# Transposing Q, K and x in the DMA crossbar instead of on TensorE, in an attention-and-feed-forward kernel

## The chip, the cores and the metric

One core of one Trainium2 chip. The metric is the time of one execution in device microseconds (us), median of several executions. Every timed series ran together with the kernel before on the same chip, and ratios compare only those runs. Some executions fall into a slower state (a lower granted TensorE clock, over 1.5% above the fastest of the same kernel). They are marked slow and left out of ratios.

The views of the profile use short names: PE is TensorE (PEld its weight loads), DVE is VectorE, ACT is ScalarE, POOL is GpSimd, SP is SyncE, which issues transfers. "Crossbar" stands for the transposing transfer that `dma_start_transpose` asks of the DMA engines. The span is the time from the first to the last instruction of a profiled execution. The granted clock is the share of TensorE's full speed that was allowed.

## The reference

Four batches of eight heads, 768 tokens, head size 64. Attention is causal with a window of 128 keys plus four sink keys; the result goes through a feed-forward stage with three first-layer matrices joined by a maximum.

```python
keep = is_sink | in_window                 # n_sink = 4, window = 128
a = softmax(where(keep, q @ k.T / sqrt(64), -1e9))
x = (a @ v) as [3072 tokens, 512]
h = maximum(maximum(x @ w1, x @ w2), x @ w3)    # 512 -> 768
out = h @ w_out                                 # 768 -> 512
```

Inputs and output are float32; the kernel computes in bf16 with float32 sums.

## The kernel before

The tokens are cut into 12 chunks of 256 (three per batch). A software pipeline runs in the loop: iteration i does the first layer and output of chunk i, the attention of chunk i+1, the K and Q preparation of chunk i+2, and it issues the load of chunk i+3. The order on every engine is the order in which the program emits instructions; the program asks for no scheduler. The parts that the change touches:

```python
def prep(ci, j, g):                       # K (j=0) or Q (j=1), 4 heads
    x = bfs[ci]                           # bf16, cast by GpSimd
    pt = ps_o.tile([128, 2, 2, 128], BF16, tag="o", name="pt")
    for i in range(2):
        for p in range(2):
            nc.tensor.transpose(..., x[:, j, g, i, p * 128:(p + 1) * 128], ident)
    if j == 1:                            # Q: ACT copies out of PSUM
        put(nc.scalar.copy, qT[...], slice(0, 128))
    else:                                 # K: DVE copies each head of a pair into
        for h in range(2):                # its own half of kz, rest of kz is zero
            put(nc.vector.tensor_copy, kz[...][:, 2 * g:2 * g + 2, h], hp)
        if c == 0 and b > 0:
            sink_k(b, g)                  # DVE copies the sink keys of a new batch
# ... (cut)
def xpose(ci, t):                         # x, 128 tokens
    for ds in range(DS):                  # DS = 4
        nc.tensor.transpose(pt[:, ds], x[:, ds * 128:(ds + 1) * 128], ident)
    nc.scalar.copy(xTs[ci][:, :, t * 128:(t + 1) * 128], pt)
# ... (cut)
for i in range(2, NCH):                   # letter, chunk (a=i, b=i+1, c=i+2), index
    cast(i + 2)                           # GpSimd
    load(i + 3)                           # SyncE: 6 to 10 DMAs
    run("Sb0 Fa0 Sb1 Fa1 Sb2 Fa2 Sb3 Kc0 Fa3 Zb Sb4 Fa4 Ab00 Sb5 Qc0 Fa5 Ab01 Sb6 Kc1 Fa6 "
        "Sb7 Qc1 Fa7 Fa8 Ab10 Ab11 Ya0 Tb0 Tb1 Ya1", a=i, b=i + 1, c=i + 2)
```

S is the score of one head, F one of nine groups of eight first-layer matmuls, Z the scores against the sink keys, A attention times V, T the transposes of x, Y the output with its store, K and Q the preparation above. Sink keys are the first four keys of a batch, which every query sees; they are kept in a tile of their own, ks.

The softmax here doesn't subtract the row's maximum and nothing guards it: scores larger than these inputs give would overflow.

## Time and profile before

| | kernel before |
|---|---|
| time of its first three runs | 211.73 us (211.26 to 212.39) |
| span of the profiled run, granted clock | 208.2 us, 1.00 |
| TensorE (PE) busy | 191.0 us, 92% |
| loop, first h matmul of chunk 3 to that of chunk 11 | 123.4 us, 15.4 per iteration |

How to read it: the prediction below shows the lines that make PE the bound. Two more views are needed. First, the queues of the DMA engines from the page (packets, MB, then the time that the packets took as a share of 16 engines over the span; in a table by stretch a packet counts where it starts, so that a share there can pass 1):

```profile
q1 hardware_dynamic: 73984, 25.21, 47.8%
```

Second, the timeline of SyncE, which issues nearly all transfers, over one iteration (start, duration, destination and source, count):

```profile
102.86 0.36 SPq L329 DMA_DIRECT2D out_dram<-y_sb  x1
103.31 1.20 SPq L80 DMA_DIRECT2D qk_raw<-in_k_dram  x2
...
107.90 1.24 SPq L85 DMA_DIRECT2D v_raw<-in_v_dram  x2
115.42 2.54 SPq L329 DMA_DIRECT2D out_dram<-y_sb  x2
```

SyncE issues ten loads in 5.8 us and is then idle for 6.3 us, until the next stores.

### The profile page before, as it was taken

The page shows a single profiled execution, that of the slowest core. Times are in us where ns is not written, and L with a number is a line of the kernel's source. Part 1 is how long each engine was busy: PE and PEld are TensorE (multiplying, and loading weights), DVE is VectorE, ACT ScalarE, POOL GpSimd, SP SyncE. Part 2 cuts the span into 40 slices and gives each one's busy share as a digit, 9 for nine tenths or more (in the row PEclk, how much of TensorE's full clock was granted, in tenths as well). Part 3 has the DMA queues.
Part 4 walks back from the last instruction along what each step waited for, and adds up shares of the span by engine and source line. Part 5 has one row for each costly group of instructions (what it writes and reads, how often), then busy time and mean ns, then how long its engine had stood idle before and what let it go on. Part 6 is the DMA issues. An engine that isn't in the chain of part 4 may idle for free.

```text
span 208.2 us, 5083 instructions
## 1 busy us (share of the span) xinstructions
PE 191.0 (92%) x2027; PEld 155.2 (75%) x2039; DVE 131.2 (63%) x289; ACT 117.0 (56%) x216; POOL 66.1 (32%) x110
## 2 busy tenths in 40 slices
PE   7664879899899999999999999999999999999992
PEld 7553768785687798688587798798687797796870
DVE  3787516995488288299288288298299288276250
ACT  8766751444763764764653764764653863863412
POOL 6289119978245143025024043024025000000000
PEclk9999999999999999999999999999999999999998
DMA  5999996972999393385295392392284200200202
GB/s 135 231 264 203 215 258 115 242 170 103 209 280 220 121 219 69 107 181 117 76 220 115 116 228 63 113 229 65 102 193 111 104 0 3 101 5 0 104 0 101
DMA packets 76391, 28.67 MB, mean 138 GB/s; under 512 B 65872, under 2 KB 73296, under 8 KB 76368
## 3 DMA queue, kind: packets, MB, share of 16 engines
q1 hardware_dynamic: 73984, 25.21, 47.8%
q0 software_dynamic: 2384, 3.15, 8.9%
q8 instruction: 16, 0.26, 0.6%
q14 instruction: 7, 0.06, 0.1%
HBM read 25.20 MB, written 6.29 MB: 151 GB/s over the span
## 4 chain that ended last, share of the span: by engine, by line
PE 68%; DVE 18%; ACT 9%; issue 2%; POOL 0%; DVEq 0%; POOLq 0%; ACTq 0%
PE h_ps L313 37%; PE y_ps L324 9%; DVE h_sb L319 6%; DVE e_sb L254 6%; DVE x_sb L289 4%; ACT e_sb L251 4%; PE st L244 4%; PE pt L207 4%; PE o_ps L281 3%; PE xt_ps L301 2%; PE warm L117 2%; PE st L245 2%; ACT h_sb L317 2%; PE sk L260 2%; PE st L242 1%
## 5 line engine op out<-in xcount | busy, mean ns | idle before, releaser
L313 PE MATMUL h_ps<-xT,w 128*128 128x256 bf16 x864 | 107.9, 273 | 0.7 <-ACT xT L302 0.7
L313 PEld LDWEIGHTS <-w 128*128 128x128 bf16 x864 | 81.1, 98 | 9.5 <-issue 0.8
L251 ACT ACTIVATE e_sb<-st 128x512 bf16<-128x512 f32 (+1 forms) x96 | 53.6, 565 | 23.5 <-PE st L245 23.5
L319 DVE TENSOR_TENSOR h_sb<-h_sb,h_ps 128x512 bf16<-128x512 bf16 x72 | 49.4, 686 | 18.0 <-PE h_ps L313 15.1
L254 DVE TENSOR_TENSOR e_sb<-e_sb,msk 128x1024 bf16<-128x1024 bf16 (+1 forms) x48 | 33.7, 703 | 41.1 <-ACT e_sb L251 40.9
L186 POOL CAST qk_bf<-qk_raw 128x512 bf16<-128x512 f32 x36 | 24.6, 688 | 68.8 <-DMA qk_raw<-in_k_dram 49.6
L327 ACT COPY y_sb<-y_ps 128x512 f32<-128x512 f32 x24 | 14.1, 586 | 35.9 <-PE y_ps L324 32.9
L324 PE MATMUL y_ps<-wo,h_sb 128*128 128x512 bf16 x132 | 33.1, 379 | 0.7
L317 ACT CAST h_sb<-h_ps 128x512 bf16<-128x512 f32 x36 | 21.1, 586 | 17.1 <-PE h_ps L313 16.9
L244 PE MATMUL st<-qT,kz 128*128 128x256 bf16 x96 | 25.8, 273 | 2.0 <-DVE kz L215 1.0
L324 PEld LDWEIGHTS <-h_sb 128*128 128x128 bf16 x144 | 12.5, 98 | 12.7 <-DVE h_sb L319 2.7
L289 DVE TENSOR_TENSOR x_sb<-o_ps,rc 128x256 bf16<-128x256 f32 x48 | 20.4, 425 | 1.7
L245 PE MATMUL st<-qT,kz 128*128 128x128 bf16 x96 | 20.9, 219 | 0.0
L281 PE MATMUL o_ps<-ve,e_sb 128*128 128x65 bf16 x352 | 18.6, 193 | 1.9 <-DVE e_sb L254 1.9
L190 POOL CAST ve<-v_raw 128x512 bf16<-128x512 f32 x24 | 15.6, 656 | 12.9 <-DMA v_raw<-in_v_dram 12.7
L281 PEld LDWEIGHTS <-e_sb 128*128 128x128 bf16 x352 | 16.6, 97 | 3.8 <-DVE e_sb L254 2.5
L207 PE MATMUL pt<-ident,qk_bf 128*128 128x128 bf16 x192 | 18.3, 221 | 1.2 <-DVE kz L213 0.6
L215 DVE COPY kz<-pt 64x512 bf16<-64x512 bf16 x40 | 16.7, 418 | 3.4 <-PE pt L207 3.0
L207 PEld LDWEIGHTS <-qk_bf 128*128 128x128 bf16 x192 | 12.7, 99 | 2.9 <-issue 1.2
L242 PE MATMUL st<-qT,kz 128*128 128x128 bf16 x64 | 14.0, 219 | 0.0
L302 ACT COPY xT<-xt_ps 128x512 bf16<-128x512 bf16 x24 | 13.3, 595 | 0.8 <-PE xt_ps L301 0.8
L244 PEld LDWEIGHTS <-kz 128*128 128x128 bf16 x96 | 9.4, 98 | 3.7 <-DVE kz L215 1.3
(48 smaller groups left out, 135.4 us busy)
## 6 DMA issues: line engine op xcount, KB each, us to landing
v_raw<-in_v_dram SPq DMA_DIRECT2D x24, 256.0 KB, 4.3
out_dram<-y_sb SPq DMA_DIRECT2D x24, 256.0 KB, 2.0
qk_raw<-in_k_dram SPq DMA_DIRECT2D x40, 128.0 KB, 2.8
qk_raw<-in_q_dram SPq DMA_DIRECT2D x36, 128.0 KB, 2.8
w<-in_moe_w_dram POOLq DMA_DIRECT2D x3, 768.0 KB, 11.3
qk_raw<-in_q_dram SPq DMA_DIRECT2D x6, 256.0 KB, 4.2
qk_raw<-in_k_dram SPq DMA_DIRECT2D x4, 256.0 KB, 4.2
wo<-in_moe_w_out_dram POOLq DMA_DIRECT2D x2, 384.0 KB, 5.6
```

The source lines that it names most:

```text
L186: eng.tensor_copy(bfs[ci][:, j, g].rearrange("p i x -> p (i x)"), qk[:, j, g])
L207: nc.tensor.transpose(pt[:, i, p] if runs else pt[:, p, i], x[:, j, g, i, p * 128:(p + 1) * 128], ident)
L244: nc.tensor.matmul(st[:, 1:3], lhsT=kh[:, 0:128], rhs=qh, start=True, stop=True)
L245: nc.tensor.matmul(st[:, 3], lhsT=kh[:, 128:256], rhs=qh[:, 128:256], start=True, stop=True)
L251: nc.scalar.activation(e[:, h, lo:], st[:, lo:], AF.Exp, scale=scale)
L254: nc.vector.tensor_tensor(out=e[:, :, lo:], in0=e[:, :, lo:], in1=m, op=ALU.mult)
L281: nc.tensor.matmul(o[:, hh], lhsT=es[ci, p][:, h, sl], rhs=ve[b % 2][:, n, 2 * p + h], start=(c == 0 and x == 0), stop=(x == len(blocks) - 1),
L289: nc.vector.tensor_mul(xs[ci, t][:, 4 * g:4 * g + 4], o[:, :, 0:D], rc.unsqueeze(2).to_broadcast([128, 4, D]))
L313: nc.tensor.matmul(hp[:, f], lhsT=w_sb[wi][:, ds, (2 * fp + f) * 128:(2 * fp + f + 1) * 128], rhs=xTs[ci][:, ds, :], start=(ds == 0), stop ...
L317: nc.scalar.copy(dst, hp)
L319: nc.vector.tensor_max(dst, dst, hp)
L324: nc.tensor.matmul(yp, lhsT=hs[ci][:, fb, t * 128:(t + 1) * 128], rhs=wo[:, fb], start=(fb == 0), stop=(fb == FB - 1))
```

## The change

Intent: take 24 of PE's transposes out of each iteration and give them to the DMA crossbar. K is written zero-padded in bf16 by GpSimd, so that the crossbar fills the padded tile directly and DVE's copies go as well. Queries stay in two-token order (a partition holds two neighbouring tokens, so the even tokens come first and then the odd ones), which lets Q be loaded in 512-byte runs; the stores put the rows back in place. The order of the loop is new, so that x is ready earlier.

```diff
 def cast_qk(ci, j, g, eng):
+    if j == 0 and ci >= CPB:                    # K, zero-padded, into kb
+        for h in range(2):
+            eng.tensor_copy(kb[ci % 2][:, 2*g:2*g+2, h, :, 64*h:64*h+64]..., qk[:, j, g]...)
+        return
 ...
 def prep(ci, j, g):
+    if ci >= CPB:
+        if j == 0 and g == 0:
+            nc.sync.dma_start_transpose(out=kz[...], in_=kb[ci % 2]...)      # 0.52 MB
+        elif g == 0:
+            nc.sync.dma_start_transpose(out=qT[...], in_=bfs[ci][:, 1]...)   # 0.26 MB
+        return
-        if c == 0 and b > 0:
-            sink_k(b, g)
 def sink_score(ci):
+    if c == 1 and b > 0:                        # sink keys copied directly ahead of Z
+        for g in range(2):
+            sink_k(b, g)
 def xpose(ci, t):
+    if ci >= CPB:
+        nc.sync.dma_start_transpose(out=xTs[ci][:, t], in_=xs.pop((ci, t))...)
+        return
 def ffn_y(ci, t):
-    nc.sync.dma_start(out=out[r0:r0 + 128], in_=y)
+    for i in range(2):
+        nc.sync.dma_start(out=...[i], in_=y[64 * i:64 * i + 64])
 # entry of the loop
+run("Kd0 Qd0", d=3)
 load(4)
-run("Ac10 Ac11 Yb0 Tc0 Kd0 Tc1 Qd0 Yb1 Kd1 Qd1", b=1, c=2, d=3)
+run("Ac10 Ac11 Yb0 Tc0 Tc1 Yb1", b=1, c=2)
 # loop: cast(i + 2); load(i + 3); then
-    run("Sb0 Fa0 Sb1 Fa1 Sb2 Fa2 Sb3 Kc0 Fa3 Zb Sb4 Fa4 Ab00 Sb5 Qc0 Fa5 Ab01 Sb6 Kc1 Fa6 "
-        "Sb7 Qc1 Fa7 Fa8 Ab10 Ab11 Ya0 Tb0 Tb1 Ya1", ...)
+    run("Kc0 Qc0 Sb0 Fa0 Sb1 Sb2 Fa1 Sb3 Zb Sb4 Fa2 Sb5 Ab00 Fa3 Sb6 Ab01 Sb7 Fa4 Fa5 Ab10 "
+        "Tb0 Ab11 Tb1 Fa6 Fa7 Fa8 Ya0 Ya1", ...)
```

Cut: masks and score operands for the two-token order, K of chunks 1 and 2 loaded in 256-byte instead of 512-byte runs, the clearing of kb in place of kz.

## The prediction

> **What bounds the kernel now.** I read the engine shares first, then the table by stretch cut at the iterations of the steady loop, then the timeline of one iteration, then the groups of what is removed, and last the waits and the queue of SyncE, because the new transposes are issued there.
>
> ```profile
> PE 191.0 (92%) x2027; PEld 155.2 (75%) x2039; DVE 131.2 (63%) x289; ACT 117.0 (56%) x216; POOL 66.1 (32%) x110
> ...
> 117.20:132.90 15.70, 15.54 (x173) 12.97 (x173) 10.10 (x22) 9.54 (x19) 4.29 (x6) 1.00 0.54 135
> 132.90:148.70 15.80, 15.60 (x172) 12.76 (x172) 10.90 (x26) 9.45 (x19) 4.04 (x6) 1.00 0.54 134
> 148.70:163.30 14.60, 14.28 (x150) 11.54 (x150) 9.90 (x22) 8.43 (x18) 4.04 (x6) 1.00 0.58 144
> ```
>
> The last three lines are one iteration each of the loop (span, then busy us of PE, weight loads, DVE, ACT, POOL, then granted clock, DMA share, GB/s). PE is busy for all but 0.2 to 0.3 us of each, at full clock. Busy could still hide waits, so I check it against what PE must stream. In the chain of waits eight h matmuls of 256 columns take 0.87 us, that is 109 ns each, and six of 512 columns 1.29 us. In the timeline one head's scores take 0.22 us and one group of nine attention matmuls 0.44. An iteration whose attention chunk is not the first of its batch then needs 9 x 0.87 (h) + 8 x 0.22 (scores) + 0.44 (sink scores) + 4 x 0.44 (attention) + 2 x 1.29 (y) + 16 K and Q transposes at 0.055 (0.88) + 8 x transposes (0.44) = 15.7 us. Measured: 15.7 and 15.8. So the loop (55.0 to 193.6 us, nine such iterations) is bound by PE's issue, and 1.32 us of each is transposes.
>
> ```profile
> L207 PE MATMUL pt<-ident,qk_bf 128*128 128x128 bf16 x192 | 18.3, 221 | 1.2 <-DVE kz L213 0.6
> L301 PE MATMUL xt_ps<-ident,x_sb 128*128 128x128 bf16 x96 | 9.6, 221 | 2.6 <-DVE x_sb L289 1.3 <-ACT xT L302 0.7
> L215 DVE COPY kz<-pt 64x512 bf16<-64x512 bf16 x40 | 16.7, 418 | 3.4 <-PE pt L207 3.0
> L302 ACT COPY xT<-xt_ps 128x512 bf16<-128x512 bf16 x24 | 13.3, 595 | 0.8 <-PE xt_ps L301 0.8
> PE sk L260 <- DVE ks L229: 2.8, 1, 2.8
> POOL qk_bf L186 <- DMA qk_raw<-in_k_dram: 49.6, 15, 9.9
> 118.05 1.00 SPq L80 DMA_DIRECT2D qk_raw<-in_k_dram  x2
> out_dram<-y_sb SPq DMA_DIRECT2D x24, 256.0 KB, 2.0
> ```
>
> The 221 ns of a transpose is its pipeline length, not its cost: pieces of the chain show eight in 0.45 us. The 2.8 us is the only long PE wait: the first sink score waits for DVE's sink-key copies. POOL waits only for loads, so casts run an iteration ahead. A SyncE issue of a load takes 0.5 us, of a store 0.36.
>
> **What the Trainium skill says.** "VectorE: DVE Perf Modes", section "The three transpose paths", gives 390 ns for a 128x128 transpose on TensorE and 1309 ns through the DMA crossbar: worse by latency, but on another unit. "TensorE: Matmul & The Clock Gate", section "Part 4: PE-mode transpose", has about 275 ns in a kernel; the trace has 221, and only 55 in occupancy. "DMA: Bandwidth & Descriptors", section "Latency and other measured facts", has 261 GB/s for a DMA transpose. No transfer in the trace before is a transpose; its plain loads in 256-byte packets reach 229 GB/s at a DMA share of 0.99, which is near it. The same page, "Issuing engines are not separate DMA queues": all DMAs share 16 engines, so transposes queue among the loads; the trace agrees in that loads land in 2.8 us alone and 14 at worst.
>
> **The change, part by part.**
>
> PE: the order of instructions has 432 fewer on PE, 216 transposes with their weight loads: 9 chunks x 16 (K, Q) and 9 x 8 (x). 216 x 0.055 = 11.9 us, all on the bound, plus about 0.1 us of waiting for x per iteration. With no new wait the floor is 14.4 us for an ordinary iteration and 13.0 for one whose chunk begins a batch: 6 x 14.4 + 3 x 13.0 = 125.4 us where the loop now has 138.6. This is the most that the loop can give, 13 us.
>
> DVE and ACT: per chunk four kz copies of 0.42 (1.7 us) and two qT and two xT copies of 0.59 (2.4 us) go. Neither engine is the bound, so this only gives slack.
>
> DMA: K padded is 0.52 MB, Q 0.26, x 0.26: 1.05 MB per chunk, an estimate of 4.0 us at the skill's 261 GB/s. Now 0.54 x 15.7 = 8.5 us of an iteration's DMA time are taken; Q in 512-byte runs saves perhaps 0.6. About 12 of 14.5 us: full, not over.
>
> SyncE: 8 loads of 0.5, 4 stores of 0.36, 4 transposes. If a transpose holds the sequencer about as long as its data moves plus 0.4 us, that is 4.1 + 1.4 + 5.6 = 11 us per iteration. It fits, but in order: the x transposes stand behind loads, K and Q.
>
> New waits from the new order. I laid out one iteration by hand with the durations above (exp 0.61, h cast and y copy 0.49 effective on ACT; mask and max 0.69 on DVE). The scores are now bunched (S0 F0 S1 S2 F1 S3 Z S4) on two PSUM buffers. ACT frees itself from the y copy at 0.7 us, then exp, cast, exp, exp, exp end at 1.3, 1.8, 2.4, 3.0 and 3.6. The sink score wants its buffer at 2.7 and gets it at 3.1, S4 at 3.7: PE waits **0.6 us**; 0.3 where there is no sink. In the second chunk of a batch it is worse: the sink-key copies, done ahead with the K transposes before, now stand directly ahead of Z, and on DVE behind the mask of heads 2 and 3, which needs exp 3 (3.6): mask to 4.35, four copies 0.6, Z at 5.0. PE waits 2.7 to 5.0: **2.3 us**, three times.
>
> x transposes: the second attention group ends at 9.8, DVE (behind two maxima) delivers x at 10.8 and 11.4, and next F0 wants xT at 15.2: 3.8 us for issue and landing. A store needs 2.0 and a 128 KB load 2.8. In a chunk that begins a batch everything is 1.6 us earlier on PE but not on SyncE; I take 0.5 us of wait there.
>
> Loop: 125.4 + 3 x 0.6 + 3 x 2.3 + 3 x 0.3 + 3 x 0.5 = 136.5, against 138.6: **-2.1**. Most of the 13 us is given back.
>
> Before the loop: 16 transposes of chunk 3 fewer (-0.9); the sink copies of batch 0 are emitted earlier, which takes most of the 2.8 us wait, of which I count 1.0 since the weights are loading at a DMA share over 1; contiguous instead of scattered kz and qT copies (418 for 727 ns) in two chunks, -0.5; K of chunks 1 and 2 back to 256-byte packets in a DMA-full phase, +0.5. Entering the loop, SyncE must issue chunk 3's transposes before load 4, so loads start some 4 us later and K of chunk 4 and the first x come late: +1.0. Sum -0.9. In all 211.7 - 2.1 - 0.9 = 208.7. The hand layout is likelier to be too strict than too loose, as the author has visibly placed x early to hide the transposes, so I go to **207.8 us**.
>
> **Rivals.** (1) Full gain: the waits by ACT and DVE are absorbed, PE stays busy, 199 to 203 us. For it: PE-bound by the count above, DVE and ACT lose 4 us per chunk. Against it: the fixed order of DVE ahead of Z, which nothing can absorb. (2) SyncE or the DMA ring becomes the bound: a transpose moves at half of 261 GB/s or holds the sequencer for twice its data; then x lands 2 to 4 us late in every iteration, 218 to 230 us. For it: loads of 6 us stand ahead in the same ring, the DMA share is already 0.99 for the first half of an iteration. Against it: K and Q have a whole iteration of slack, only x is urgent. (3) My middle: PE waits replace PE work, 205 to 211. (4) The two-run reading of q and xT slows the moving side of matmuls: matmul rows would show over 109 ns per 256 columns; I know of nothing for it.
>
> **Range and chances.** Rival 1 has about a quarter, the middle a half (half of it under 207.5, the limit of faster by 2%), rival 2 a quarter, of which a part stays under 216. Range 199.5 to 218. Faster 0.46, same 0.33, slower 0.21.
>
> **What would show it.** Right: PE rows lose 216 transposes; the iterations take about 15.0, 16.7 and 13.8 us in turn; the waits list has PE sk or its weight load waiting for DVE ks for about 2.3 us three times, and PE st for ACT e_sb. x transposes land in under 3.8 us, and h_ps waits for the DMA of xT under 1 us per iteration. Wrong: h_ps waiting for xT by more than 2 us each time (rival 2), with x transposes landing in over 5 us; or PE busy over 98% in the loop with iterations of 14.4 and 13.0 (rival 1), which would mean that my layout of ACT and DVE was wrong.

## The result

| | before | after |
|---|---|---|
| median | 212.06 us (211.26 to 215.24, 4 runs) | 235.88 us (230.19 to 241.29, 4 runs) |
| ratio of fast runs | 1 | 1.094 (95%: 1.076 to 1.112) |

Ratios are the mean time of one kernel's fast runs over that of the other's of the same rounds, so not quite the ratio of the medians quoted. The four executions of the change took 230.2 and 233.2 us (fast) and 238.6 and 241.3 us (slow). The result is correct, and slower by 9.4%.

The changed kernel's profile fell on a slow execution (238.6 us, clock 0.92). I use it here for the kind and place of the waits, and only after finding the same waits in fast profiles of nearly the same kernel (entry and loads-behind-x below). The table by stretch, first five loop iterations and the ninth (columns as in the prediction: span; busy PE, weight loads, DVE, ACT, POOL; clock; DMA share; GB/s):

```profile
63.80:85.25 21.45, 14.91 (x126) 11.11 (x125) 8.48 (x18) 6.93 (x14) 8.20 (x16) 0.82 0.93 216
85.25:103.19 17.94, 15.70 (x148) 12.25 (x150) 9.20 (x22) 7.17 (x14) 4.19 (x8) 0.93 0.94 177
103.19:119.70 16.51, 14.68 (x146) 11.50 (x148) 8.87 (x18) 7.73 (x15) 4.55 (x8) 1.00 0.96 191
119.70:135.60 15.90, 13.15 (x125) 10.21 (x127) 8.15 (x18) 6.44 (x13) 4.25 (x8) 1.00 0.98 200
135.60:155.40 19.80, 17.78 (x148) 13.44 (x150) 10.07 (x22) 6.54 (x13) 4.39 (x8) 0.83 0.70 159
...
207.30:221.70 14.40, 14.24 (x148) 11.44 (x147) 8.71 (x18) 7.53 (x14) 0.00 (x0) 1.00 0.25 56
```

At full clock PE's own work is what was predicted: 14.7 and 14.2 us of busy time (14.4 predicted), 13.15 where a chunk begins a batch (13.0 predicted). Only the last line, an iteration without loads and without K and Q, takes that time. The others take 15.9 to 21.5 us. In the first four the DMA share is 0.93 to 0.98 where it was 0.54 to 0.58; the fifth, at 0.70, has a clock of 0.83 and a wait of 1.8 us for the sink keys. So PE's own work is no longer the bound. The waits of PE:

```profile
PE h_ps L335 <- DMA xT<-x_sb: 10.0, 6, 2.3
PE o_ps L291 <- POOL vs L174: 6.5, 1, 6.5
PE st L256 <- DMA qT<-qk_bf: 5.5, 2, 4.2
PE sk L277 <- DVE ks L243: 5.1, 4, 1.8
PE st L258 <- DMA qT<-qk_bf: 4.1, 1, 4.1
```

PE, which waited once for 2.8 us, now waits for x (10.0 us in all), for Q (9.6), for the sink keys (5.1), and 6.5 us once at the start. What do x and Q wait for? SyncE's timeline of one iteration answers to the one shown of before:

```profile
118.44 2.47 SPq L352 DMA_DIRECT2D out_dram<-y_sb  x4
120.97 1.18 SPq L80 DMA_DIRECT2D qk_raw<-in_k_dram  x2
...
124.39 2.09 SPq L85 DMA_DIRECT2D v_raw<-in_v_dram  x2
126.58 3.63 SPq L216 DMA_TRANSPOSE kz<-kb  x1
130.30 1.25 SPq L220 DMA_TRANSPOSE qT<-qk_bf  x1
131.66 2.58 SPq L316 DMA_TRANSPOSE xT<-x_sb  x2
134.32 2.47 SPq L352 DMA_DIRECT2D out_dram<-y_sb  x4
```

From store to store it is 15.88 us and there is no pause: 2.5 us of stores, 5.5 of loads, 3.6 for K, 1.25 for Q, 2.6 for x. Work comes out in that order, so K is issued 7 us into an iteration, behind a load whose data is not cast before the next iteration, and x is last. The queue of the DMA engines:

```profile
q1 hardware_dynamic: 104992, 34.65, 67.8%
```

67.8% of 236.9 is 160.6 us. The variant without crossbar (below) took 48.9% of 218.2 = 106.7 us with otherwise the same transfers. The difference, 53.9 us for 9 chunks of 1.05 MB, is **6.0 us of engine time per chunk, or 175 GB/s**. The packets of the trace say the same: the change has 36864 more of 256 bytes than the variant without crossbar, at 23.4 ns each, where the variant's own 256-byte packets, loads, took 18.2.

The split stores cost engine time too: their 2048-byte packets took 139 ns each, 26.7 us in all, where the whole stores of before took 88 ns, 17.0 us in all. That is 0.8 us per chunk for the same bytes.

Against the second profile of before (span 212.9 us) the 24.0 us lie as follows (one slow execution and one whose state is unknown, so this tells where and not exactly how much): +3.5 up to chunk 2's first h matmul, +6.4 in its iteration (21.5 against 15.1), +13.5 from chunk 3's to chunk 11's (136.4 against 122.9), +0.5 in the last. At the entry of the loop SyncE shows why:

```profile
54.56 2.62 SPq L352 DMA_DIRECT2D out_dram<-y_sb  x4
57.28 3.25 SPq L216 DMA_TRANSPOSE kz<-kb  x1
60.63 1.24 SPq L220 DMA_TRANSPOSE qT<-qk_bf  x1
61.93 1.12 SPq L80 DMA_DIRECT2D qk_raw<-in_k_dram  x2
...
75.94 3.49 SPq L216 DMA_TRANSPOSE kz<-kb  x1
```

GpSimd had K of chunk 3 ready at 48.5 us; its transpose went out at 57.28, behind chunk 0's stores, and load 4 behind that, at 61.93 (50.74 before). K of chunk 4 then had to wait for load 5: 75.94.

Part of PE's timeline in the iteration from 135.6 us (start, duration, in brackets the wait ahead):

```profile
133.90 0.22 PE L256 MATMUL st<-qT,kz 128*128 128x128 bf16 x1 [1.33 <-DMA qT<-qk_bf]
...
135.59 1.82 PE L335 MATMUL h_ps<-xT,w 128*128 128x256 bf16 x8 [1.31 <-DMA xT<-x_sb]
...
141.60 0.39 PE L277 MATMUL sk<-qT,ks 128*128 128x256 bf16 x2 [1.78 <-DVE ks L243]
...
142.74 1.91 PE L335 MATMUL h_ps<-xT,w 128*128 128x256 bf16 x8
```

Eight h matmuls that take 0.87 us at full clock took 1.8 to 1.9 here, the first eight behind two waits of 1.3 us, the others behind a wait of 1.8: half speed. The table by stretch, cut where the granted clock changes (columns as above; the clock is the third number from the end), shows what went ahead:

```profile
132.25:135.67 3.42, 0.78 (x6) 0.30 (x5) 0.00 (x0) 1.18 (x2) 0.00 (x0) 1.00 0.60 125
135.67:139.08 3.41, 3.41 (x19) 2.57 (x19) 0.51 (x1) 1.57 (x3) 0.00 (x0) 0.50 0.84 192
139.08:142.49 3.41, 1.45 (x14) 0.85 (x12) 2.50 (x7) 0.60 (x1) 1.86 (x3) 1.00 0.93 241
142.49:145.91 3.42, 3.42 (x26) 2.67 (x25) 0.85 (x2) 1.57 (x3) 2.39 (x5) 0.50 1.22 266
```

PE was busy 0.78 of 3.42 us from 132.25 us, and 1.45 of 3.41 us from 139.08; each time the next 3.41 us had a clock of 0.50.

The same working over all profiles but the one at a clock of 0.65, with the stretch laid at the changes of the clock: no full-clock stretch of 3.41 us with PE idle for under 47% of it was followed by half clock, and every one idle for over 58% was. In between both occur. (The ends of matmuls are modelled in the profile, so these shares are rough.) So in these profiles it is the idle time in a stretch that counts, and two short waits add up.

### The profile page after: what moved, and what is told of

The parts are those of the page before. It is cut to its first block, busy times and chain, and to the rows that moved or that the text cites. A ratio compares the mean times of both kernels' runs of the same rounds, so it can differ in the third digit from the quotient of the medians.

```text
span 236.9 us, 4670 instructions
## 1 busy us (share of the span) xinstructions
PE 192.2 (81%) x1811; PEld 150.5 (64%) x1823; DVE 115.6 (49%) x253; ACT 97.9 (41%) x180; POOL 65.6 (28%) x124
## 3 DMA queue, kind: packets, MB, share of 16 engines
q1 hardware_dynamic: 104992, 34.65, 67.8%
## 4 chain that ended last, share of the span: by engine, by line
PE 56%; DMA 15%; SPq 14%; POOL 5%; ACT 4%; issue 3%; DVE 1%; POOLq 0%; ACTq 0%; DVEq 0%
PE h_ps L335 34%; PE y_ps L346 8%; DMA xT<-x_sb 6%; SPq L80 6%; PE st L258 4%; PE o_ps L299 3%; DMA qk_raw<-in_k_dram 3%; ACT e_sb L265 3%; DMA qk_raw<-in_q_dram 3%; SPq L316 2%; SPq L75 2%; DMA v_raw<-in_v_dram 2%; PE st L259 2%; PE sk L277 2%; POOL kb L437 2%
## 5 line engine op out<-in xcount | busy, mean ns | idle before, releaser
L335 PE MATMUL h_ps<-xT,w 128*128 128x256 bf16 x864 | 113.3, 286 | 10.7 <-DMA xT<-x_sb 10.0
L335 PEld LDWEIGHTS <-w 128*128 128x128 bf16 x864 | 85.4, 103 | 24.6 <-issue 12.2
L265 ACT ACTIVATE e_sb<-st 128x512 bf16<-128x512 f32 (+1 forms) x96 | 51.1, 565 | 32.7 <-PE st L259 31.8
L182 POOL CAST kb<-qk_raw 128x256 bf16<-128x256 f32 x36 | 15.1, 448 | 89.6 <-DMA qk_raw<-in_k_dram 89.6
L258 PE MATMUL st<-qT,kz 128*128 128x256 bf16 x96 | 27.4, 297 | 5.6 <-DMA qT<-qk_bf 4.1
L259 PE MATMUL st<-qT,kz 128*128 128x128 bf16 x96 | 22.3, 235 | 0.0
L203 POOL CAST ve<-v_raw 128x512 bf16<-128x512 f32 x24 | 15.2, 635 | 16.3 <-DMA v_raw<-in_v_dram 15.9
L256 PE MATMUL st<-qT,kz 128*128 128x128 bf16 x64 | 14.9, 232 | 5.5 <-DMA qT<-qk_bf 5.5
L258 PEld LDWEIGHTS <-kz 128*128 128x128 bf16 x96 | 10.1, 105 | 14.1 <-DMA kz<-kb 5.5
L291 PE MATMUL o_ps<-vs,e_sink 128*128 128x260 bf16 x32 | 9.2, 286 | 6.5 <-POOL vs L174 6.5
L190 POOL CAST qk_bf<-qk_raw 128x512 bf16<-128x512 f32 x18 | 12.3, 681 | 3.1 <-DMA qk_raw<-in_q_dram 1.9
L304 DVE RECIPROCAL rc<-o_ps 128x4 f32<-128x4 f32 x48 | 8.5, 176 | 8.9 <-PE o_ps L299 8.9
L259 PEld LDWEIGHTS <-kz 128*128 128x128 bf16 x96 | 10.2, 106 | 2.1 <-issue 1.8
## 6 DMA issues: line engine op xcount, KB each, us to landing
qk_raw<-in_k_dram SPq DMA_DIRECT2D x48, 128.0 KB, 2.6
out_dram<-y_sb SPq DMA_DIRECT2D x48, 128.0 KB, 2.3
```

The lines of the kernel that those rows point to most:

```text
L182: eng.tensor_copy(kb[ci % 2][:, 2 * g:2 * g + 2, h, :, 64 * h:64 * h + 64] .rearrange("p a i d -> p i a d"), qk[:, j, g].rearrange("p (i a ...
L203: eng.tensor_copy(ve[b % 2][:, 2 * c + n, :, 0:D], raws[ci][1][:, n])
L258: nc.tensor.matmul(st[:, 1:3], lhsT=kh[:, 0:128], rhs=qh, start=True, stop=True)
L259: nc.tensor.matmul(st[:, 3], lhsT=kh[:, 128:256], rhs=qh[:, 1], start=True, stop=True)
L265: nc.scalar.activation(e[:, h, lo:], st[:, lo:], AF.Exp, scale=scale)
L335: nc.tensor.matmul(hp[:, f], lhsT=w_sb[wi][:, ds, (2 * fp + f) * 128:(2 * fp + f + 1) * 128], rhs=xTs[ci][:, :, ds], start=(ds == 0), stop ...
```

## The experiments

Every run gave the right result. "x" is the ratio of fast runs to the kernel before of the same rounds, with its 95% interval. The theory at first: **SyncE's queue in order and the DMA engines are the new bound** (rival 2 of the prediction). Its rivals: the late sink copies, the start-up, the bunched order.

### K of chunks 1 and 2 in 512-byte runs again

```diff
-                    if j == 1:
+                    if j == 1 or ci in (1, 2):
```

> The changed kernel with K of chunks 1 and 2 loaded in 512-byte runs again, as before the change, and put in order by the PSUM copy; nothing else differs. Theory: in the changed kernel the first sink attention matmul waited 6.5 us for POOL, which waited for V of chunk 1, which landed late (cast at 24.2 us, before the change at 16.5) because K of chunk 1 in 256-byte packets held the DMA engines until the weights came; chunk 2's K transposes then stood at 43.1 us instead of 36.5. If so, this run loses the wait for POOL, has chunk 2's transposes near 37 us and is 5 to 8 us faster than the changed kernel (about 225). Rival: the late V comes from something else (chance in the DMA, the run of 0.9 clock at the start): then the time stays within 2 us of the changed kernel's.

Measured: 234.29 us, x 1.084 (1.073 to 1.095). The single wait for vs fell from 6.5 to 3.4 us and the first K transpose of chunk 2 came at 40.0 instead of 43.1 us, but the profile was a slow one, its loop took 136.6 us (136.4), and the time moved by about 1%, within the intervals. The start is a small part.

### x on TensorE, K and Q on the crossbar

```diff
-            if ci >= CPB:            # in xpose
+            if ci >= NCH:
-    ... Sb7 Fa4 Fa5 Ab10 Tb0 Ab11 Tb1 Fa6 Fa7 Fa8 Ya0 Ya1
+    ... Sb7 Fa4 Fa5 Fa6 Fa7 Fa8 Ab10 Ab11 Ya0 Tb0 Tb1 Ya1
```

> The changed kernel with the x transposes of all chunks on TensorE and ScalarE again (8 matmuls and 2 copies per chunk), placed between the two y blocks as before; K and Q stay on the crossbar. Theory A: the loop is bound by SyncE's in-order queue, 15.9 to 16.5 us of issues per iteration with x last in it, and PE waits for x (1 to 2.5 us) and then runs at a lower clock. Then without x (2.6 us) SyncE needs 13.5 us, PE no longer waits for xT, iterations fall to 14.9 to 15.5 us save for those with the sink copies, and the time is 12 to 18 us below the changed kernel's. Rival B: the crossbar transposes as such fill the DMA (share 0.94 to 0.98): K and Q are three quarters of the bytes, so then PE waits for kz and qT in place of x and the gain is under 5 us.

Measured: 234.11 us, x 1.092 (1.081 to 1.104). All waits for the transfer of x are gone, four of the iterations take 14.6 to 15.0 us, and the loop took 129.3 us instead of 136.4. Yet the total hardly moved: 4 us at the entry waiting for Q, a bad start (chunk 2's first K transpose at 48.5 us, 43.1 in the change), the sink waits as before. Taking one wait away is not enough.

### K and Q on TensorE, x on the crossbar

```diff
-            if j == 0 and ci >= CPB: ...   # in cast_qk and prep
+            if j == 0 and ci >= NCH: ...
```

> The changed kernel with K and Q transposed on TensorE again in all chunks (two-token order kept, no padded K, halves zeroed at the start as before), x alone on the crossbar and given as early as in the changed kernel. Theory A (SyncE's queue): without K and Q (4.8 us of issue) SyncE needs about 11.5 us, x transposes go out as soon as x is there, land in 2.4 us and PE does not wait; iterations 15.2 to 16 us, total 10 to 16 us below the changed kernel's. Theory B (x transposes are too slow whatever stands ahead of them): PE still waits 1 us or more for xT in most iterations and the gain is under 5 us.

Measured: 227.71 us, x 1.064 (1.055 to 1.072). The waits for x fell from 10.0 to 1.2 us although x itself is untouched. So x was late because K, Q and the loads stand ahead of it, not because its own transpose is slow (issue to landing 2.4 us here and in the change). The profile was a slow one, and its loop, with 16 transposes back on PE, took 136.5 us, as in the change. New are longer sink waits (2.4 to 2.8 us, three times) and 4.0 us of attention waiting for DVE's K copies.

### Loads from chunk 4 on issued by GpSimd

```diff
-            eng = nc.sync
+            eng = nc.sync if ci < 4 else nc.gpsimd
```

> The changed kernel with the loads from chunk 4 on issued by GpSimd instead of SyncE: same bytes, same transposes. It tells SyncE's issue time from the DMA engines' time. If the queue of SyncE is what binds (5.3 to 5.8 us of its 16 per iteration are loads), SyncE idles again, the x transposes go out when x is ready, and the time falls by 8 to 15 us. If the 16 DMA engines bind (share 0.94 to 0.98 in the loop), the share stays above 0.9, the iterations stay near 16 us and the time changes by less than 4 us. GpSimd may be slow at issuing short runs; then POOL's casts come late and the time rises.

Measured: 240.16 us, x 1.127 (1.118 to 1.137), slower than the change. Two iterations:

```profile
88.20:105.20 17.00, 14.46 (x148) 11.51 (x150) 9.06 (x22) 7.16 (x14) 12.37 (x20) 1.00 1.10 195
121.00:141.30 20.30, 13.52 (x125) 10.29 (x127) 8.30 (x18) 6.36 (x13) 9.36 (x15) 0.87 1.16 157
```

SyncE was relieved of some 6 us per iteration and the iterations did not get shorter; the DMA share rose over 1 and K took 11.1 us from issue to landing (5.6). SyncE's time to issue alone is thus not the limit. That the loads then compete with the urgent transposes in the engines themselves fits these numbers, but GpSimd, which also casts, was busy longer too (12.4 and 9.4 us of these two iterations, 4.2 to 4.6 in the change), and the run doesn't part the two.

### The weights behind V of chunk 1

```diff
-        load_w(0) ... load_w(1) load_w(2) load(2, nc.gpsimd)    # ahead of cast_v(1, ...)
+        cast_v(1, ...); load_w(0); load_w(1); load_w(2); load(2, nc.gpsimd)
```

> The changed kernel with one reorder on GpSimd: the weight loads are issued after the casts of V of chunk 1, so after its landing. In the traces, from the moment the weights stream on the software queue (about 15 us) the hardware queue moves 0.02 to 0.18 MB per 3 us until they end at 31 us, and what of chunk 1 has not landed by then waits: V was cast at 16.5 us in the kernel before, at 24.2 in the changed one, 21.3 in e1, 29.5 in e2. Theory: this cliff, and not K's short runs as such, is the loss at the start. Then V of chunk 1 is cast by 17 us, PE no longer waits for POOL at the first sink attention, chunk 2's first K transpose stands at 38 us or earlier (43.1, 40.0, 48.5 so far), and the time is 3 to 7 us below the changed kernel's. Rival: the weights themselves then come 2 us later and the first h matmuls wait for them, no gain.

Measured: 237.37 us (no ratio, too few fast runs). V of chunk 1 was cast at 17.4 and 18.3 us instead of 17.8 and 24.2, but the weights' packets ran to 35.4 us instead of 30.8 and the first cast of chunk 2 came at 36.1 instead of 31.5. The wait was shifted, not removed, as the rival said.

### Sink copies early again

```diff
-            if c == 1 and b > 0: sink_k ...    # ahead of Z of the second chunk
+            elif ci: sink_k ...                # at Z of the first chunk of the batch
```

> The changed kernel with the sink-key copies of batches 1 to 3 emitted one iteration earlier, in the chunk that begins the batch, instead of directly ahead of the sink score. Theory: PE waits for DVE's ks copies 1.6 to 2.0 us in three iterations, and twice the clock dropped after it; so this takes away those waits, iterations 3, 6 and 9 fall by 2 to 4 us each and the time by 5 to 10 us. Rival: SyncE and the DMA engines set the iteration's length anyway (the queue was issuing without a pause), so PE waits for xT in place of ks, and the time falls by less than 3 us.

Measured: 237.5 us, x 1.125 (1.112 to 1.138). The sink waits are gone (the iterations concerned take 16.1 and 15.8 us instead of 19.8 and 18.4), the loop took 130.0 us instead of 136.4, and the start was worse by 4 us; the total did not fall (the ratio of the change was 1.094).

### Chunk 3's transposes and load 4 directly behind the casts

```diff
         cast(3)
+        run("Kd0 Qd0", d=3)
+        load(4)
         ...
-        run("Kd0 Qd0", d=3)
-        load(4)
```

> The changed kernel with the crossbar transposes of chunk 3 and load 4 emitted right after chunk 3's casts, ahead of the first stores in SyncE's order. In the changed kernel they stood behind stores that wait for ScalarE until 57 us, PE waited 4.1 us for qT of chunk 3, load 4 was issued at 61.9 us (before: 50.7) and the x transposes of chunk 3 came late (PE waited for xT until 85 us, clock 0.82). Theory: this order cost some 8 to 10 us between 55 and 85 us; then this run has no wait for qT at chunk 3, iteration 2 takes 16 to 18 us instead of 21.5, and the time falls by 5 to 10 us. Rival: SyncE and the DMA are behind as a whole, the loss is only shifted into later iterations, gain below 3 us.

Measured: 233.51 us, x 1.110 (1.100 to 1.120). The loop began at 57.9 instead of 63.8 us, and its first iteration then took 22.7, with one wait of 7.2 us for Q of chunk 4. SyncE's timeline of this profile, a fast one:

```profile
60.01 5.71 SPq L352 DMA_DIRECT2D out_dram<-y_sb  x8
65.77 1.20 SPq L80 DMA_DIRECT2D qk_raw<-in_k_dram  x2
...
71.26 3.57 SPq L216 DMA_TRANSPOSE kz<-kb  x1
```

K of chunk 4 was cast by 61.8 us, but load 5 stood ahead of it (65.8 to 71.2). The gain was lost to the next thing in the queue.

### The load behind the x transposes

```diff
-            if i + 3 < NCH:
-                load(i + 3)
             run("Kc0 Qc0 Sb0 ... Tb0 Ab11 Tb1", ...)
+            if i + 3 < NCH:
+                load(i + 3)
             run("Fa6 Fa7 Fa8 Ya0 Ya1", a=i)
```

> The changed kernel with the load of an iteration emitted behind its x transposes in SyncE's order; all bytes and transposes the same. If the order in the queue is what makes x late (order theory), the x transposes go out as soon as DVE has x, PE no longer waits for xT in the loop, and iterations fall to about 15 us where they are 16.5 and 15.9, 5 to 12 us in all. If the total of the DMA engines binds (throughput theory: 15.5 of 16 us taken), x is on time but the loads and with them K and Q come late instead: PE waits for kz or qT, the DMA share stays at 0.95, and the time stays within 4 us.

Measured: 230.9 us, x 1.096 (1.087 to 1.105). The loop took 130.0 instead of 136.4 us, waits for x 4.7 instead of 10.0, and K's issue 2.0 instead of 3.5 us at the median, with no load just ahead of it. The late entry and a bad start (chunk 2's first K transpose at 45.8 us) remained.

### No crossbar at all, the rest of the change kept

```diff
-            if ci >= CPB:     # in cast_qk, prep, xpose; loop order of before
+            if ci >= NCH:
```

> Everything of the change but the crossbar: two-token order on chip, loads and stores as in the changed kernel, sink copies ahead of the sink score, but K, Q and x transposed on TensorE in the old loop order. Theory: apart from the start (some 3 to 8 us, where K of chunk 1 in short runs lets V of chunk 1 fall behind the weights) the loss of 20 us is the crossbar's and its order's. Then the loop from F3 to F11 takes 123 to 128 us here (before 123.4, changed 136.4), the clock stays near 1.0 in it, and the time is 214 to 221 us. Rival: the two-token reads of q and xT, split stores or the sink copies cost the loop by themselves: then F3 to F11 takes over 130 us.

Measured: 222.15 us, x 1.020 (1.007 to 1.032). Its loop has three waits of 1.4 to 1.7 us for the sink keys and is otherwise that of before (127.5 against 122.9; iterations without such a wait 14.5 to 15.6). So the two-token order and the split stores cost little where the DMA engines have time to spare; the crossbar, with the order of the loop that came with it, brought most of the loss.

### All repairs together: x on TensorE, and x on the crossbar

```diff
+ K of chunks 1 and 2 in 512-byte runs; sink copies early; entry and load order as above
+ K through the crossbar unpadded (0.26 MB), DVE copies the halves into kz:
+   nc.sync.dma_start_transpose(out=kts[ci]..., in_=bfs[ci][:, 0]...)
+   nc.vector.tensor_copy(kz[...][hp, :, h]..., kts[ci][hp])
```

> A version meant to keep the gain: K and Q through the crossbar but K without padding (0.26 MB instead of 0.52; two DVE copies put its halves into kz), x on TensorE, scores spread as before, sink copies a chunk earlier, chunk 3's transposes and load 4 ahead of the stores, K and Q ahead of the load in the queue, K of chunks 1 and 2 in long runs. Theory: the DMA engines bind the changed kernel at 15.4 to 16 us per iteration; its transposes took 6.8 us of them (1.05 MB), here about 3.5 us, so the DMA needs some 12 us and PE (14.9 and 13.5 us of issue) binds again: F3 to F11 takes 115 to 120 us and the time is 203 to 209 us. If the crossbar disturbs PE in some other way, the loop stays above 123 us and the time above 211.

Measured: 211.87 us, x 0.983 (0.972 to 0.994).

> The same with x through the crossbar too, ahead of the load in the queue, and the changed kernel's bunched order. Theory: DMA about 13.5 us per iteration, PE floor 14.4 and 13.0 plus 0.6 us where ScalarE holds the score buffers; x lands in 2.4 us if nothing stands ahead of it: F3 to F11 takes 114 to 122 us. If x waits behind earlier loads still draining, PE waits for xT over 1 us in several iterations and it is slower than e10.

Measured: 212.31 us, x 0.990 (0.982 to 0.997). One iteration of it:

```profile
120.30:135.40 15.10, 14.56 (x151) 11.62 (x150) 9.76 (x20) 7.55 (x15) 4.37 (x6) 1.00 0.83 177
```

So the loss of 9% is not the price of the crossbar as such: with order, sink copies, runs of K and padding repaired it is gone. But the gain is not there either: the loop takes 122.2 to 122.4 us, as before. PE now waits for DVE instead (8.8 us in all for the maxima of h, which stand behind K's copies in DVE's order).

A caution on both ratios: in these rounds two executions of the kernel before are slow (215.6 and 216.7 us), and the ratios are reached only with them. The fast runs alone average 213.5 us, against 212.4 for x on the crossbar (0.995) and 211.2 for x on TensorE (0.990). The variant without crossbar ran in the same rounds: 218.9, or 1.025.

> The kernel before once more, for a second profile of its start: if the cliff between the weights' queue and the loads is a race, V of chunk 1 may miss it here too, with chunk 2's first K transpose later than 36.6 us; if the start is the same to 0.5 us, the kernel before clears it with some reserve.

The kernel before once more, one run: 214.73 us, span 212.9, which gave the second profile of before used above. Chunk 2's first K transpose stood at 41.4 us instead of 36.6, and PE waited 3.6 us for vs, which it did not in the first profile. So the kernel before can lose time at this place too, and a late start is not the change's alone.

### K unpadded, alone

```diff
+ K through kts as above, in the changed kernel; nothing else
```

> The changed kernel with one thing different: K goes through the crossbar unpadded (0.26 instead of 0.52 MB per chunk), and DVE then copies its two halves into the padded tile. If the bytes of the transposes on the DMA engines set the length of an iteration: 0.26 MB less is about 1.5 us of engine time per chunk (6.0 us for 1.05 MB, from the queue shares of the changed kernel and of the variant without crossbar), over seven iterations with loads some 8 to 10 us: 225 to 228 us. If SyncE's issue in order or the order of instructions sets it and the bytes do not: the same number of transposes, 0 to -4 us, 232 to 236, and more waits for DVE.

Measured: 238.49 us, x 1.118 (1.108 to 1.127). No gain, against my theory, although the DMA share of the iterations fell to 0.70 to 0.84. K's transposes still went out 7 to 8 us into the iteration, behind the load, and DVE's copies then waited for them with the maxima that PE needs behind them: PE waited for those up to 4.0 us at a time in the loop, 6.7 in its first iteration and 21.4 in all. Its waits for x and Q (10.0 and 9.6 us in the change) were gone, and SyncE paused for 1.8 to 2.8 us in the two iterations looked at. So the run does not show that fewer bytes do nothing: it took one kind of wait away and brought another, because the copies that unpadded K needs are a second change. **While the order holds the transposes back, whatever stands behind them waits.** Full DMA engines alone are not the explanation.

### All repairs, K padded

```diff
- K unpadded
+ K padded in kb, as in the change
```

> The repaired kernel (K unpadded, sink copies early, loads behind x, K of chunks 1 and 2 in 512-byte runs, entry order, x on the crossbar; 212.3 us) with the padding of K put back and nothing else. If the bytes are what the repair gained most by: +8 to +14 us, 220 to 226, DMA share of the loop near 1.0 again. If the order and the start were what it gained by: within 3 us of 212.3.

Measured: 216.65 us, x 1.017 (1.010 to 1.024). Two iterations, the first of the loop and one further on:

```profile
58.80:71.70 12.90, 12.84 (x128) 10.21 (x127) 8.27 (x22) 6.24 (x13) 1.15 (x2) 1.00 0.74 160
104.60:120.40 15.80, 13.50 (x128) 10.29 (x126) 8.81 (x22) 7.36 (x15) 4.23 (x8) 1.00 1.06 199
```

Both have the same work for PE. Where the DMA engines are at 0.74, the iteration takes 12.9 us, PE's floor (13.0 predicted); at 1.06 it takes 15.8, and PE waits there for Q (1.5 us) and its weight loads for x (0.8). With the order repaired the transfers are the bound, and the padding, less what the copies cost without it, is worth 2.0 to 2.7% (216.7 against 212.3 us in medians; 1.017 against 0.990, or 0.995 with fast runs alone).

### Filler matmuls in the waits

```diff
+            if i == 2: warm(60)
             run("Sb0", b=i + 1)
+            if i < 9: warm(24)
             run("Fa0 Sb1 Sb2 Fa1 Sb3", a=i, b=i + 1)
+            if (i + 1) % CPB == 1: warm(24)
             run("Zb ...", a=i, b=i + 1)
```

> The changed kernel with filler matmuls of 128 columns at the three places where TensorE was seen to wait: 60 at the entry of the loop, 24 ahead of the first h matmul while there are loads, 24 ahead of the sink scores of a batch's second chunk (0.055 us each, 1.3 us per 24). If the lower granted clock follows from TensorE's own waits and costs time: granted clock above 0.97 over the span instead of 0.92 to 0.955, 2 to 8 us faster than 235.9. If it comes from elsewhere, or the iterations are as long as their DMA whatever the clock: clock unchanged or the time the same or up to 6 us longer.

Measured: 238.0 us, no ratio (three of four runs slow). In the profile the iteration that had a clock of 0.83 shows

```profile
138.30:155.70 17.40, 17.02 (x197) 14.23 (x197) 9.22 (x22) 7.45 (x14) 3.96 (x8) 1.00 0.95 184
```

1.00, and the one that had 0.90 is at 1.00 too; the loop took 132.7 instead of 136.4 us (135.6 to 136.6 in three other profiles with this loop, those of the runs of K, the weights and the entry). The clock of the span rose only to 0.957, short of the 0.97 expected, since start and one later wait were not covered and the entry was longer than its filler, and a worse entry ate the rest. The lower clock follows from PE's own waits, and in this profile it cost the loop some 4 us: a consequence that adds to the loss, not its root. The time of the whole kernel did not show it.

### The two repairs of order together

```diff
+ entry and load order as above, in the changed kernel; nothing else
```

> The changed kernel with the two repairs of order together that gained 2.4 and 5.0 us alone: chunk 3's transposes and load 4 directly behind the casts of chunk 3, and the load of chunk i+3 behind the x transposes; K padded, sink copies late, K of chunks 1 and 2 in 256-byte packets as in the change. If the order on SyncE's queue is the larger part of the loss and the two repairs need each other (the early entry lost its gain to K of chunk 4, which stood behind load 5): 216 to 223 us, the first iteration about 13 to 15 us without a wait for qT. If they only add up: 227 to 230. If the repaired kernel with padding (216.7) owed its gain to the sink copies and the runs of K: 228 or more.

Measured: 221.89 us, x 1.049 (1.043 to 1.055). Alone they had reached 1.110 and 1.096, where the change is at 1.094; together 1.049. The profiled execution ran at a clock of 0.65, so the kernel was run once more:

> The kernel of f4_order once more for a profile at an ordinary clock, as its profiled execution ran at a clock of 0.65: 219 to 224 us; first iteration of the loop 13 to 15 us long with no wait for qT over 1 us; the waits that are left are the sink copies (three of 1.6 to 2.2 us) and x (up to 2 us per iteration).

Measured: 217.65 us, a single run at a clock of 0.98, 4 us below the fast runs of the same kernel just above (220.7 to 222.1 us, clocks 0.93 to 0.96). Its profile thus shows a better execution than that ratio. Its first iteration and its longest waits:

```profile
57.00:72.80 15.80, 13.25 (x129) 10.25 (x127) 8.15 (x18) 7.42 (x15) 3.29 (x6) 1.00 0.85 188
```

```profile
PE h_ps L335 <- DMA xT<-x_sb: 6.8, 6, 2.0
PE sk L277 <- DVE ks L243: 5.6, 3, 2.0
```

K of chunk 4 now went out at 65.0 us instead of 71.3 in the entry variant, and the first iteration took 15.8 us instead of 22.7: chunk 3's first h matmul came at 72.8 us, in the change at 85.3. The loop from there took 128.0 us (136.4). SyncE still issued without a pause in the stretch that I looked at (59 to 109 us). The queue's 74.4% of 215.9 is again 160.6 us: the engines' time is the same in a run whose loop loses 5.1 us on that of before instead of 13.5, so it does not grow with the waits. It is not wholly a constant of the transfer: x alone on the crossbar (51.7% of 229.4 us, less 106.7) comes to 198 GB/s by the same working. The expected 13 to 15 us for the first iteration was missed by 0.8, one wait for Q was 1.3 us where at most 1 was expected, and the remaining waits are as expected.

### The best variant again

> The best variant so far, once more and unchanged (K unpadded and Q on the crossbar, x on TensorE, repaired order; 211.9 us, ratio 0.9825). If its lead is real: ratio below 1 with the whole interval, 0.975 to 0.995. If it was the luck of one chip: the interval holds 1.

Measured: 212.04 us, x 1.001 (0.996 to 1.006). The lead of 1.8% did not hold. The best variant (x on TensorE) and the kernel before are the same within the noise; x on the crossbar was not run again.

## Why the prediction was wrong

It named 207.8 us, a gain; the time was 235.9. By its steps:

**PE's work: right.** Iterations without a wait take 14.4 us, and 12.9 where a chunk begins a batch, as predicted. The floor was there, and only iterations without DMA pressure reached it.

**SyncE "fits": wrong, and the main step that failed.** The prediction had 11 us per iteration (1.4 for stores, 4.1 for loads, 5.6 for transposes). Measured was 15.9 without a pause: 2.5, 5.5 and 7.5. It saw that "the x transposes stand behind loads, K and Q", but allowed x 3.8 us and K and Q "a whole iteration of slack". Neither held, as the queue was never empty: K went out 7 us into each iteration and x 12 to 15. x then landed 2.4 us after its issue, well inside the 3.8 us: what the prediction left out is the wait ahead of the issue. Putting load i+3 behind the transposes and chunk 3's transposes ahead took the ratio from 1.094 to 1.049. Moving some 6 us of loads from SyncE to GpSimd had won nothing (x 1.127), so SyncE's time to issue alone was not it.

**Entry of the loop: right cause, wrong size.** "K of chunk 4 and the first x come late: +1.0." It cost some 10 us up to chunk 3's first h matmul (85.3 against 72.8 with the order repaired, of which 2.7 were there already at chunk 2's first K transpose), since one late transpose delays the next load, its cast and the next transpose.

**DMA time: right kind, wrong size.** The estimate of 4.0 us per chunk at 261 GB/s was 6.0, at 175 GB/s. The split stores, which the prediction counted on SyncE and not on the engines, add 0.8. So "about 12 of 14.5 us: full, not over" became 15.6 of 15.9 (0.98). Unpadding K in the repaired kernel was worth 2.0 to 2.7%; in the unrepaired one the copies that come with it ate whatever it gave.

**Sink copies: right.** Predicted 2.3 us three times, measured 1.6 to 2.0; together with the runs of K they are worth up to 3.2% (1.049 to 1.017). Their profiles, the first of them the single run at a clock of 0.98, show less: loops of 128.0 and 127.2 us, spans of 215.9 and 214.3.

**Bunched scores: too strict.** 0.6 us per iteration was allowed on top of 14.4; the iteration without DMA pressure took 14.36 in all.

**Not foreseen: the clock.** After waits of 1.3 us and more TensorE ran at half rate for a while. Filling the waits brought the clock back in most of the loop, and 4 us of it.

In ratios the loss divides into 4.5% order on SyncE, 3.2% sink copies and runs of K, and 2.0 to 2.7% padding of K, which leads from 1.094 to 0.990 (0.995 with fast runs alone). These are differences between runs of different rounds, so the parts are rough, and the sequence matters: K unpadded alone gained nothing (x 1.118), and neither repair of order alone lowered the ratio.

**Rivals.** Rival 2, that SyncE or the DMA engines become the bound, came true in kind, and it had a quarter of the chances; the time lies above its range of 218 to 230 us. Its reasons held in part: a transpose moved at two thirds of 261 GB/s and not at half, x came late, but no transpose of x landed in over 5 us, as its sign had it. "K and Q have a whole iteration of slack" was the argument against it, and this failed. Rival 4, slower matmuls from the two-token order, is refuted: the kernel without crossbar has iterations of before, and the median of an h matmul in the change is 273 ns, as before.

**Open.** How much of SyncE's 15.9 us is its own work and how much is being held up by transfers still under way can't be read off: K's issue took 3.6, 2.0 or 1.3 us depending on what was ahead and on its bytes. The start differs by 3 to 8 us among variants and by 5 between two profiles of the kernel before; what decides it was only partly traced (the weights in the DMA engines between 15 and 31 us).

## What to carry to other kernels

Moving work to an idle unit moves it into that unit's queue: before counting the gain, write down the whole queue of the issuer for one iteration, in order, and ask for each urgent entry what stands ahead of it. Prefetches belong behind transfers that are needed next. And when several limits coincide, single repairs can show nothing, as here; their combination, and then taking single ones away from it, tells more of what each is worth.

## What the Trainium skill lacked or had wrong

- "DMA: Bandwidth & Descriptors", section "Latency and other measured facts", gives 261 GB/s for a DMA transpose with a non-contiguous middle dimension, and more for a contiguous one. Here transposes of bf16 tiles from SBUF to SBUF took 6.0 us of engine time for 1.05 MB beside loads: 175 GB/s (53.9 us for 9.4 MB), and 198 GB/s for x alone.
- No page that I read says how long the issuer is held by a transpose beside other transfers; "DMA: Bandwidth & Descriptors" gives sequencer cycles of a transpose only in a comparison made for a later chip, without the transfer. Here, in the change, SyncE was held 1.2 us at the median for 128x512 elements of x (2.3 at most), 1.25 for 0.26 MB of Q (2.1 at most) and 3.5 for 0.52 MB of K (1.8 to 4.4); with loads no longer just ahead K's median was 2.05. Landing was 2.4 us after issue for x at the median, 3.2 for Q, 4.8 to 5.6 for K.
- "TensorE: Matmul & The Clock Gate", section "Part 1: The HAM clock gate (the "warmup" mystery)", speaks of an idle window of about 3.4 us ahead of the lower clock. The clock here does change in steps of 3.41 us, but the window need not be idle: windows with PE busy for 0.78 and 1.45 us of 3.4 were followed by half clock, and over the profiles the line lies at 47 to 58% idle. Three single waits of 1.4 to 1.7 us in the variant without crossbar left the clock at 1.00. (Further down in the same part the page does tell of a kernel whose short idles lowered the clock, without saying how much idle it takes.)
